# One 512 KB broadcast load per pair, or four of 128 KB: the spread inverses of path A

## The chip, the cores and the metric

The kernel runs on one core of a Trainium2 chip. The metric is device time in microseconds (us) of a whole execution; lower is better. The core has five instruction streams: TensorE (PE, matmuls), VectorE (DVE), ScalarE (ACT), GpSimd (POOL) and SyncE (SP). In this kernel SP issues all the transfers, and 16 DMA engines carry them.

## What is computed

Two attention layers over the same input (2048 tokens, width 448, 16 heads of 28) are mixed by a gate. The change touches the first one, path A, at its last division:

```python
# path A, per head h: linear attention with a softmax feature map
phi_q = concat(softmax(q @ w_phi), softmax(-(q @ w_phi)))     # 56 features
phi_k = concat(softmax(k @ w_phi), softmax(-(k @ w_phi)))
num = phi_q @ (phi_k.T @ v)
den = phi_q @ phi_k.sum(axis=tokens) + 1e-6
o   = num / den                       # the change is in how 1/den is spread
a   = concat_heads(o) @ wo
# path B: full softmax attention of the same input, b
out = g * a + (1 - g) * b             # g = sigmoid(x . gate_w)
```

## The kernel before

Everything is float32; most products are split into a high and a low part (three passes of matmuls). The program has three stretches. The first (to about 205 us) projects q and k of path B and accumulates keys and values of path A. The second (205 to about 350 us) finishes path A: 16 token tiles of queries (`pq`), their features, the numerators, the division, the output projection (`poa`), and then the values of path B (`pvb`). The third (350 us to the end) is path B's softmax attention. Matmuls of a running maximum (`pmd`, `pmb`, line 260, which ACT and DVE reduce at lines 264 and 265) are spread through the second stretch.

PE, DVE, ACT and POOL run in the order in which the Python code emits instructions. SP is not on that list: the library's scheduler sets the order of the transfers. Each transfer signals its completion on one of eight semaphore lanes, DMAHW0 to DMAHW7, taken in turn; a transfer whose lane is still held by an unfinished one waits at SP, and all behind it wait too.

Path A's division works on pairs of token tiles, `tb` = 0 to 7, 256 tokens each. Per pair:

- `numer` (PE, line 529) makes two tiles `pn` of 128 partitions by 512. Rows 32j to 32j+27 are a head's numerators, row 32j+28 its denominators. ACT copies them to `oUa` (`normalize1`, line 381).
- SP takes the four rows of denominators of each tile out of `oUa` into the small tile `dena` (line 384), so that many partitions hold them.
- `normalize2`: DVE takes the reciprocals (line 389); SP writes them to the DRAM tile `rda`, 4 rows of 1024 numbers (line 393), and loads `rda` back into `rsa`, 128 partitions of 1024 numbers, each of the four rows spread over 32 partitions (line 394). This load is what is changed.
- `normalize3`: DVE multiplies `oUa` by `rsa` (line 400). `normalize4`: ACT makes the high part of the result `oTa` (line 408), POOL the low part (line 409). `out_a` (line 538) projects it.

The loop at line 703 places these steps: the step with line 389 comes two turns after line 381, and line 400 two turns after that, with other work of DVE between. `rsa` has two buffers, `oUa` three. Path B uses the same functions with n = 1 (`rsb`, one tile, 256 KB), where line 400 runs on POOL.

Of the kernel before, what the change touches and what calls it, by code (L numbers as in the profile page):

```python
# [41 lines left out]
def gated_mix_kernel(ctx, tc, xT, wqkB, wvB, wvA, wkAT, wqAT, phi, woA, woB,  # L42
# [7 lines left out]
    nc = tc.nc  # L50
# [336 lines left out]
    def normalize2(pool, oU, den, nm, n):  # L387

        nc.vector.reciprocal(den, den)
        rd = dr.tile([4, n * 512], F32, tag=f"rd{n}", name=f"rd{nm}", bufs=2)  # L390
        rs = pool.tile([P, n, 512], F32, tag="rs", name=f"rs{nm}", bufs=n)
        for k in range(n):
            nc.sync.dma_start(rd[:, k * 512:(k + 1) * 512], den[:, k, :])
        nc.sync.dma_start(rs.rearrange("p n q -> p (n q)"),
                          rd.unsqueeze(1).to_broadcast([4, 32, n * 512]))
        return oU, rs

    def normalize3(oU, rs, n):
# [304 lines left out]
    for i in range(2 * NT + 11):  # L703
        t, q = i, i - NT
# [44 lines left out]
        if y >= 6 and y % 2 == 0 and tb - 3 < 8:  # L749
            num[tb - 3] = normalize2(ta, *num[tb - 3], f"a{tb - 3}", 2)  # L750
# [293 lines left out]
    def finish(gq, s):  # L1044
# [8 lines left out]
        def f2():  # L1053
            st["n"] = normalize2(late_p, *st["n"], f"b{gq}", 1)
# [189 lines left out]
```

## Time and profile before

| | us |
|---|---|
| median of 3 runs | 977.87 (977.84 to 979.14) |
| the profiled execution, whole | 978.57 |
| its span, first to last instruction | 976.8 |
| PE busy | 969.2 (99%) |
| ACT busy | 751.8 (77%) |
| DVE busy | 715.7 (73%) |
| POOL busy | 227.8 (23%) |
| 16 DMA engines, mean share | 27% |

The granted clock of TensorE is 1.0 throughout. A span is read from the first to the last instruction, and what the runtime adds around it (978.57 less 976.8, 1.77 us) is in the run's time. "Idle before" in the rows below is time in which an engine had nothing running, with what ended it behind the arrow; a chain of waits follows the program back from its last instruction to whatever released each step. "SPq" marks SP's issue of a transfer, so its duration is issue and not movement.

### The profile page before, as it was taken

How to read it: one execution, taken by the hardware profiler on the slowest of the kernel's cores; microseconds unless marked ns; L12 is line 12 of the kernel's file. 1: busy time of each engine (PE TensorE's matmuls, PEld its weight loads, DVE VectorE, ACT ScalarE, POOL GpSimd, SP SyncE). 2: the span in 40 equal slices, each digit the busy share in tenths (PEclk: the TensorE clock that was granted, in tenths of full speed). 3: DMA queues.
4: the chain of work that ended last, by engine and by line, in shares of the span. 5: the costliest groups of instructions: out<-in, count | busy, mean ns of one | idle time of the engine just before them, and what ended most of it. 6: DMA issues, size and time to landing. Idle time of an engine off the chain costs nothing.

```text
span 976.8 us, 22541 instructions
## 1 busy us (share of the span) xinstructions
PE 969.2 (99%) x8510; PEld 600.1 (61%) x8510; DVE 715.7 (73%) x1338; ACT 751.8 (77%) x1442; POOL 227.8 (23%) x236
## 2 busy tenths in 40 slices
PE   9999999999999999999999999999999999999998
PEld 8777877787777655555555555545555555555555
DVE  5567767788845678888888888888888888885112
ACT  4455655577865688989888898888988989887662
POOL 1135445577634800021001001011011011010010
PEclk9999999999999999999999999999999999999999
DMA  8873110023233333021132021122231222100441
GB/s 305 303 259 118 40 53 33 29 58 94 73 108 109 101 111 132 26 59 53 57 94 74 30 61 49 59 78 69 65 83 46 65 59 72 34 21 32 143 151 57
DMA packets 56140, 84.49 MB, mean 86 GB/s; under 512 B 17216, under 2 KB 23984, under 8 KB 56032
## 3 DMA queue, kind: packets, MB, share of 16 engines
q1 hardware_dynamic: 56032, 83.06, 27.1%
q8 instruction: 67, 1.10, 0.4%
q14 instruction: 41, 0.34, 0.1%
HBM read 54.86 MB, written 27.78 MB: 85 GB/s over the span
## 4 chain that ended last, share of the span: by engine, by line
PE 91%; DMA 5%; DVE 2%; ACT 1%; issue 1%; SPq 0%; DVEq 0%; ACTq 0%
PE g L863 29%; PE pv L1008 27%; PE pqk L109 4%; PE pk L127 4%; PE pva L127 4%; PE g L288 4%; PE poa L109 3%; PE pmd L260 3%; PE pob L109 3%; PE pq L109 3%; PE pvb L127 2%; PE pvb L109 2%; DMA rsa<-rda 2%; DMA qkd<-ev 1%; DMA xraw<-in_xT_dram 1%
## 5 line engine op out<-in xcount | busy, mean ns | idle before, releaser
L871 ACT ACTIVATE p<-g 128x512 f32<-128x512 f32 x1020 | 525.6, 608 | 82.7 <-PE g L863 82.4
L295 DVE TENSOR_REDUCE part<-g 128x1 f32<-128x512 f32 x704 | 442.3, 684 | 84.1 <-PE g L288 80.8
L863 PEld LDWEIGHTS g<-qst,kst 32*128 32x128 f32 x3060 | 220.9, 182 | 215.4 <-DVE part L295 195.1
L863 PE MATMUL g<-qst,kst 32*128 32x512 f32 x3060 | 337.6, 419 | 0.1
L1008 PE MATMUL pv<-p,vb 128*32 128x512 f32 x2048 | 273.0, 604 | 0.0
L288 PE MATMUL g<-kc,qc 28*128 28x512 f32 x704 | 233.3, 495 | 0.0
L265 DVE CUSTOM_DVE_ANT_0 rl<-pmb,rl 128x512 f32<-128x512 f32 x160 | 103.4, 683 | 49.6 <-ACT rl L264 49.6
L400 POOL TENSOR_TENSOR oUb<-oUb,rsb 128x512 f32<-128x512 f32 x15 | 19.3, 1289 | 489.9 <-DMA rsb<-rdb 366.2
L264 ACT ACTIVATE rl<-pmd 128x512 f32<-128x512 f32 x160 | 87.3, 601 | 31.1 <-PE pmb L260 29.3
L288 PEld LDWEIGHTS g<-kc,qc 28*128 28x128 f32 x704 | 86.2, 181 | 0.2
L1008 PEld LDWEIGHTS pv<-p,vb 128*32 128x32 f32 x2048 | 40.5, 108 | 66.2 <-issue 64.9
L109 PE MATMUL pqk<-XH,wB 128*128 128x512 f32 x192 | 59.4, 397 | 0.8 <-DVE ev L569 0.8
L568 ACT CAST ev<-pqk 128x512 fp32r<-128x512 f32 x28 | 16.0, 589 | 38.5 <-PE pqk L109 22.5
L1019 DVE SCALAR_TENSOR_TENSOR acc<-pob,gate,acc 128x448 f32<-128x448 f32 x12 | 8.2, 684 | 48.3 <-PE pob L109 48.3
L109 PE MATMUL poa<-woA_s,oTa 128*128 128x448 f32 x192 | 43.6, 375 | 0.0
L260 PE MATMUL pmb<-kp,qp 28*128 28x512 f32 x160 | 41.7, 495 | 0.4
L109 PEld LDWEIGHTS pqk<-XH,wB 128*128 128x128 f32 x192 | 35.3, 188 | 9.9 <-issue 1.5
L569 DVE TENSOR_TENSOR ev<-pqk,ev 128x512 fp32r<-128x512 f32 x28 | 18.9, 690 | 30.5 <-ACT ev L568 30.4
L260 PE MATMUL pmd<-kp,qp 28*128 28x512 f32 x160 | 39.9, 494 | 0.0
L127 PE MATMUL pk<-wkA_s,XH 128*128 128x448 f32 x128 | 39.4, 381 | 0.0
L109 PEld LDWEIGHTS poa<-woA_s,oTa 128*128 128x128 f32 x192 | 34.8, 188 | 6.6 <-issue 2.5
L109 PE MATMUL pq<-wqA_s,XH 128*128 128x448 f32 x128 | 37.3, 374 | 0.8 <-ACT oUa L381 0.8
(158 smaller groups left out, 1052.2 us busy)
## 6 DMA issues: line engine op xcount, KB each, us to landing
qkd<-ev SPq DMA_DIRECT2D x28, 512.0 KB
qst<-qkd SPq DMA_DIRECT2D x64, 112.0 KB
kst<-qkd SPq DMA_DIRECT2D x64, 112.0 KB
od<-oTb SPq DMA_DIRECT2D x48, 112.0 KB
rsa<-rda SPq DMA_DIRECT2D x8, 512.0 KB
oL<-od SPq DMA_DIRECT2D x8, 512.0 KB
rsb<-rdb SPq DMA_DIRECT2D x15, 256.0 KB
gad<-ga SPq DMA_DIRECT2D x16, 224.0 KB
```

The lines of the kernel that those rows point to most:

```text
L109: nc.tensor.matmul(dst, l, r, start=i == 0, stop=i == len(todo) - 1)
L127: nc.tensor.matmul(dst[:, :n], l, r, start=i == 0, stop=i == len(todo) - 1, skip_group_check=True)
L260: nc.tensor.matmul(pm[j], qc[js, qt * P:(qt + 1) * P], kc[js, :], start=True, stop=True, tile_position=(32 * i, 0))
L264: nc.scalar.activation(rl, pm[i], AF.Relu)
L265: nc.vector.tensor_tensor_reduce(rl, pm[2 + i], rl, 1.0, LOWEST, ALU.add, ALU.max, part[:, col + i:col + i + 1])
L288: nc.tensor.matmul(pm, mxs[("qc", gq)][js, qt * P:(qt + 1) * P], mxs[("kc", gq // NQ, kb)][js, :], start=True, stop=True, tile_position=(3 ...
L295: nc.vector.tensor_reduce(part[:, col:col + 1], pm, AX.X, ALU.max)
L400: (nc.gpsimd if n == 1 else nc.vector).tensor_mul(oU, oU, rs)
L569: nc.vector.tensor_sub(e[:, 1, :], pq, f32(e[:, 0, :]))
L863: nc.tensor.matmul(st[j], kst_of[(gq // NQ, kt // 4)][js, k, (kt % 4) * P:(kt % 4 + 1) * P], qst_of[gq][js, q, :], start=n == 0, stop=n == ...
L871: nc.scalar.activation(p, st[j], AF.Exp, scale=SCALE)
L1008: nc.tensor.matmul(pv[32 * j:32 * j + 32, :], vb[kt // 8][:, kt % 8, 4 * g + j, :], pt[j], start=kt == 0, stop=kt == NT - 1, tile_position ...
```

## The change

For pairs (n = 2, path A alone) the load of line 394 is replaced by four loads, one per source row j: 32 copies of row j of `rda` (4 KB) go to partitions 32j to 32j+31 of `rsa`. The bytes are the same, 8 times 512 KB. Path B keeps its single load. Lines after 394 move down by five.

```diff
         for k in range(n):
             nc.sync.dma_start(rd[:, k * 512:(k + 1) * 512], den[:, k, :])
-        nc.sync.dma_start(rs.rearrange("p n q -> p (n q)"),
-                          rd.unsqueeze(1).to_broadcast([4, 32, n * 512]))
+        rows = rs.rearrange("p n q -> p (n q)")
+        if n == 2:
+            for j in range(4):
+                nc.sync.dma_start(rows[32 * j:32 * j + 32],
+                                  rd[j:j + 1].to_broadcast([32, n * 512]))
+        else:
+            nc.sync.dma_start(rows, rd.unsqueeze(1).to_broadcast([4, 32, n * 512]))
         return oU, rs
```

The order of PE, DVE, ACT and POOL stays as it was; only what they wait for is renamed. SP has 24 more transfers, and its order shifts around them. Three places matter.

SP, from pair 0's load to pair 1's (`qp` are queries for the running maximum, `dena` and `rda` as above; the brackets name the lanes and engines waited for). Before:

```order
L394 DMA rsa_2538<-rda_2537 128x1x1024 [waits DMAHW7_49,DMAHW4_49,DMAHW3_49]
L176 DMA qp_1_2800<-qkd 28x512 [waits DMAHW0_49,PE_49]
L176 DMA qp_1_2800<-qkd 28x512 x2
L393 DMA rda_2673<-dena_2570 4x32x16 [waits DMAHW5_49,DVE_49]
L393 DMA rda_2673<-dena_2570 4x32x16 [waits DMAHW6_49]
L384 DMA dena_2706<-oUa_2703 128x1x16 [waits Activation_49] x2
L176 DMA qp_1_2800<-qkd 28x512 [waits DMAHW7_49]
L394 DMA rsa_2674<-rda_2673 128x1x1024 [waits DMAHW4_49,DMAHW3_49,DMAHW0_49]
```

With the change:

```order
L397 DMA rsa_2538<-rda_2537 32x1024 [waits DMAHW7_49,DMAHW4_49,DMAHW3_49]
L397 DMA rsa_2538<-rda_2537 32x1024 [waits DMAHW0_49]
L397 DMA rsa_2538<-rda_2537 32x1024 x2
L176 DMA qp_1_2806<-qkd 28x512 [waits PE_49]
L176 DMA qp_1_2806<-qkd 28x512
L393 DMA rda_2676<-dena_2573 4x32x16 [waits DMAHW5_49,DVE_49]
L393 DMA rda_2676<-dena_2573 4x32x16 [waits DMAHW6_49]
L384 DMA dena_2712<-oUa_2709 128x1x16 [waits DMAHW7_49,Activation_49]
L384 DMA dena_2712<-oUa_2709 128x1x16 [waits DMAHW0_49,Activation_49]
L176 DMA qp_1_2806<-qkd 28x512 [waits DMAHW1_49]
L397 DMA rsa_2677<-rda_2676 32x1024 [waits DMAHW6_49,DMAHW5_49,DMAHW2_49]
```

The single load took lane 7, and the last `qp` before pair 1's load waited for that lane. Now the four take lanes 7, 0, 1 and 2, and the transfers that come next on these lanes wait for the pieces.

SP again, in the second half of the stretch, where `kt` (keys for the running maximum) stood ahead of pair 7's `rda`. Before:

```order
L176 DMA kt_1_3683<-qkd 28x512 [waits DMAHW4_49,Pool_49]
L176 DMA kt_1_3683<-qkd 28x512 [waits DMAHW5_49]
L393 DMA rda_3619<-dena_3479 4x32x16 [waits DMAHW6_49,DVE_49]
L393 DMA rda_3619<-dena_3479 4x32x16 [waits DMAHW7_49]
```

With the change:

```order
L176 DMA kt_1_3707<-qkd 28x512 [waits DMAHW1_49,Pool_49]
L393 DMA rda_3640<-dena_3500 4x32x16 [waits DMAHW2_49,DVE_49]
L393 DMA rda_3640<-dena_3500 4x32x16 [waits DMAHW3_49]
L176 DMA kt_1_3707<-qkd 28x512 [waits DMAHW4_49]
```

The second `kt`, which waited for lane 5 and with it for pair 6's load, now comes after both `rda`.

DVE, the multiplication of pair 0. Before, and then with the change:

```order
L400 TENSOR_TENSOR oUa_2458<-oUa_2458,rsa_2538 128x1024 [waits DMAHW7_49,DMAHW0_49]
```

```order
L405 TENSOR_TENSOR oUa_2458<-oUa_2458,rsa_2538 128x1024 [waits DMAHW2_49,DMAHW7_49,DMAHW1_49,DMAHW0_49]
```

The one instruction now waits for four lanes, one for each piece, where one of its two was the whole load's.

## The prediction

> **What bounds the kernel now.** I read the page's busy times and its chain first: what does PE leave idle, and does the changed load stand on the path?
>
> ```profile
> span 976.8 us, 22541 instructions
> PE 969.2 (99%) x8510; PEld 600.1 (61%) x8510; DVE 715.7 (73%) x1338; ACT 751.8 (77%) x1442; POOL 227.8 (23%) x236
> PE 91%; DMA 5%; DVE 2%; ACT 1%; issue 1%; SPq 0%; DVEq 0%; ACTq 0%
> ```
>
> PE bounds it. The chain charges `rsa<-rda` with 2%, which is two loads of 8.8 us; but PE worked through most of that, so this share is no gain. What a faster load is worth is only the PE time that its lateness costs. Who waits for it is in the list of waits of the second stretch, 205 to 325 us, and in its rows on SP (total, times, longest; the last row is the stretch itself, with the busy times of PE, its weight loads, DVE, ACT and POOL):
>
> ```profile
> DVE oUa L400 <- DMA rsa<-rda: 4.8, 3, 2.4
> ACT oTa L408 <- DVE oUa L400: 1.5, 2, 0.8
> SPq L176 <- DMA rsa<-rda: 7.7, 3, 4.7
> 205.00:325.00 120.00, 118.55 (x859) 92.41 (x839) 81.51 (x187) 87.90 (x166) 72.55 (x66) 1.00 0.27 83
> ```
>
> Three of the eight multiplications find DVE idle for the load, 4.8 us together; PE idles 120 - 118.55 = 1.45 us in the whole stretch. A matmul that waits for a buffer can also be shown as busy, so I compare the starts of PE's groups around the two long waits. Timeline of pair 0:
>
> ```profile
> 217.78 8.81 DMA rsa<-rda
> 224.52 0.18 DVE L445 TENSOR_TENSOR fsumq<-fsumq,featq 128x16 f32<-128x16 f32 x1
> 226.69 1.22 DVE L400 TENSOR_TENSOR oUa<-oUa,rsa 128x1024 f32<-128x1024 f32 x1 [1.98 <-DMA rsa<-rda]
> 227.94 1.14 ACT L408 CAST oTa<-oUa 128x512 fp32r<-128x512 f32 x2 [0.80 <-DVE oUa L400]
> 229.21 0.50 PE L260 MATMUL pmd<-kp,qp 28*128 28x512 f32 x2
> 229.63 1.10 PE L260 MATMUL pmb<-kp,qp 28*128 28x512 f32 x2
> 230.66 1.09 PE L529 MATMUL pn<-fT,KV 57*32 57x256 f32 x32
> 231.68 2.93 PE L109 MATMUL poa<-woA_s,oTa 128*128 128x448 f32 x12
> 234.45 1.03 PE L516 MATMUL pft<-ident,featq 128*128 128x128 f32 x8
> ...
> 243.80 0.51 PE L260 MATMUL pmd<-kp,qp 28*128 28x512 f32 x2
> 244.24 1.09 PE L529 MATMUL pn<-fT,KV 57*32 57x256 f32 x32
> 245.27 2.72 PE L109 MATMUL poa<-woA_s,oTa 128*128 128x448 f32 x12
> 247.82 1.03 PE L516 MATMUL pft<-ident,featq 128*128 128x128 f32 x8
> ```
>
> The last four rows are the same work undisturbed: 0.44 us from the maximum's matmuls to `pn`, 2.55 us from `poa` to `pft`. Behind the late load these are 1.45 and 2.77: **1.01 + 0.22 = 1.23 us** lost. `pmb` wanted a buffer that DVE empties after line 400. And pair 4:
>
> ```profile
> 263.54 8.83 DMA rsa<-rda
> 269.65 0.35 DVE L389 RECIPROCAL dena<-dena 128x32 f32<-128x32 f32 x1
> 272.39 1.23 DVE L400 TENSOR_TENSOR oUa<-oUa,rsa 128x1024 f32<-128x1024 f32 x1 [2.39 <-DMA rsa<-rda]
> 273.65 1.14 ACT L408 CAST oTa<-oUa 128x512 fp32r<-128x512 f32 x2 [0.70 <-DVE oUa L400]
> 274.69 1.13 ACT L519 COPY fT<-pft 128x384 f32<-128x384 f32 x3
> 275.22 0.68 PE L109 MATMUL pvb<-wvB_s,XH 128*128 128x448 f32 x2 [0.18 <-ACT fT L519]
> ```
>
> Line 408 is 0.70 us late for line 400, line 519 behind it, and PE waits **0.18 us**. Pair 1 waits 0.43 us (4.8 less the two) and costs PE nothing visible. So the lateness is worth 1.23 + 0.18 = 1.41 us, about 0.3 us of PE for each us that DVE waits.
>
> **The change, part by part.** First, how fast the load is and why.
>
> ```profile
> 222.00:223.00 1.00, 0.25 (x3) 0.01 (x1) 1.00 (x5) 1.00 (x3) 1.00 (x2) 1.00 0.82 154
> 224.00:225.50 1.50, 1.50 (x8) 1.13 (x6) 0.64 (x3) 0.50 (x2) 0.93 (x2) 1.00 0.25 101
> ```
>
> The last two columns are the mean share of the 16 DMA engines and GB/s. From 224.0 to 225.5 the big load is nearly alone: share 0.25, so four engines' worth of work, at 101 GB/s, 25 each. A microsecond after three 28-partition loads went out (222 to 223) the share is 0.82. So transfers of some 28 partitions reach most engines and the present load does not: its source is written as 4 rows by 32 copies. On this the Trainium skill's page DMA: Bandwidth & Descriptors has a rule (Why a DMA increments its semaphore by 16 and not by 1, and Rules for kernel authors): the number of engines is the largest up to 16 that divides the outermost size of both sides, so a leading 4 confines a transfer to 4. The trace's 0.25 agrees; by that rule each piece, 32 on both sides, gets 16.
>
> Landing. A spread load of about this kind is the `kt` pair:
>
> ```profile
> 316.36 0.73 SPq L176 DMA_DIRECT2D kt<-qkd  x2
> 318.29 2.65 POOL L206 TENSOR_TENSOR kp<-kp,kt 28x512 fp32r<-28x512 f32 x2 [1.96 <-DMA kt<-qkd]
> L176 SPq DMA_DIRECT2D kt<-qkd x16: 306/356/385, 43.3 to 316.7; - x16
> L394 SPq DMA_DIRECT2D rsa<-rda x8: 522/534/546, 217.8 to 297.7; - x8
> ```
>
> From the first issue to the user is 1.93 us for two of 56 KB, or about 1.57 us from the second issue. Issue costs 0.36 us (28 partitions) to 0.53 us (the present load). Four pieces: the last is issued 1.1 to 1.6 us after the first, and lands 1.6 us later, plus the time for 512 KB less the 112 KB of the pair: 400 KB at 154 GB/s is 2.7 us if nothing overlaps, nearly nothing if movement runs under the issues. That is 2.7 to 5.9 us, and I take 4 us against 8.8, because the pieces move while later ones are issued. DVE wants the data 224.70 - 217.78 = 6.9 us after the issue in pair 0 and 270.00 - 263.54 = 6.5 us in pair 4. Both ends of the estimate meet that, so all three waits go.
>
> What then is next: line 400 of pair 0 starts at 224.7, but the reduction after it needs ACT's copy at 226.15 (`pcq`), so DVE is ahead by 227.83 - 226.15 = 1.68 us, not 1.98. The second line 265 then ends at 230.17 - 1.68 = 228.5, before PE asks at 229.21. That suffices for the 1.01 us; line 409 on POOL moves up too, for the 0.22.
>
> ```profile
> 225.62 0.53 ACT L421 COPY pcq<-pq 128x448 f32<-128x448 f32 x1 [1.12 <-PE pq L109]
> 227.83 0.61 DVE L423 TENSOR_REDUCE extq<-pcq 128x16 f32<-128x448 f32 x1
> 230.10 0.08 DVE L265 DVE_READ_ACCUMULATOR2_ANT part<- 128x1 f32 x1
> ```
>
> The lost side, with the row of SP's next transfer after pair 0's load:
>
> ```profile
> 220.32 1.19 SPq L176 DMA_DIRECT2D qp<-qkd  x3
> ```
>
> 24 more issues at 0.36 to 0.53 us are 8.6 to 12.7 us of SP, 1.1 to 1.6 us per pair for whatever is queued behind: `qp`, `dena`, `rda`, `gad`. I cost this at nothing. Behind pair 0's load the next transfer goes out only at 220.32, because it waits for PE, and SP is free from 218.31; behind pair 5's, `gad` is next, whose `ga` has three buffers. Without that cover it would be 1.1 to 1.6 us on a chain, 0.5 us of PE by the ratio above. SP also gains: 7.7 us of lane waits on the long load go, so pair 1's load leaves earlier. Three more lane waits on line 400 are some 20 ns each (the event rows on DVE last 21 ns): hidden.
>
> Sum: span 976.8 - 1.4 = 975.4. That execution took 978.57 whole, while the median is 977.87; I take the difference off the median: 977.87 - 1.4 = **976.4 us**. PE is busy nearly everywhere after 235 us, so the lead should last to the end.
>
> **The rivals.**
>
> *More than the sum* (975.4). Two further rows of losses, and the row of line 400 over all pairs (shortest, median, longest; first and last start):
>
> ```profile
> 299.60 0.49 PE L260 MATMUL pmd<-kp,qp 28*128 28x512 f32 x2
> 300.45 0.67 PE L109 MATMUL pvb<-wvB_s,XH 128*128 128x448 f32 x2 [0.34 <-ACT ga L544]
> L400 DVE TENSOR_TENSOR oUa<-oUa,rsa x8: 1217/1220/1736, 226.7 to 308.5; 128x1024 f32<-128x1024 f32 x8
> ```
>
> PE loses another 0.4 us at 300.45 us, where `pvb` follows the maximum's matmuls after 0.85 us instead of 0.44, behind ACT's line 544; one line 400 took 1.74 us where 1.22 is the median. With both, 1.4 + 0.4 + 0.5 = 2.3, and some small waits on top: about 2.5. Against it: the 300.45 gap follows no wait for the load.
>
> *One row cannot feed 16 engines* (slower). Now four engines read four rows, 25 GB/s from each row; with the change 16 engines read the same 4 KB. No row of the trace shows a row read by more than one engine. If a row gave r GB/s in all, the last piece would land 524 KB / r + 2 us after the issue: 8.8 us, as now, at r = 77, so below that the change loses. At 50 GB/s it is 12.5 us, 3.7 later; the present slack of the pairs (from landing to line 400, by the issues and starts of both) is about -2.0, -0.4, 2.8, 3.0, -2.4, 1.2, 1.6, 2.0, so the added waits come to about 3 x 3.7 + 0.9 + 0.7 + 2.5 + 2.1 + 1.7 = 19 us, and at 0.3 to 0.6 us of PE each 6 to 11 us: about 986. At the 25 GB/s that one engine shows, 21 us per load would exceed the 11 us between loads, and 8 x 21 us against the 91 us from the first to the last makes some 1050. For it: identical addresses. Against it: one engine alone already drew 25 GB/s from one row without a sign of slowing.
>
> *The pieces serialize* (977.9 to 979.3). If each piece ran on the engines that the load has now, at 101 GB/s in turn, the last would land between now and 1.6 us later, and three waits longer by 1.6 cost 4.8 x 0.3 = 1.4 us. Against it stands the 0.82 of smaller transfers. The Trainium skill's page DMA: Bandwidth & Descriptors (Rules for kernel authors) says that cutting a transfer into disjoint halves of the partitions is no help, since both halves already spread over all 16 engines; its premise is not what the row of 0.25 shows of this load.
>
> *SP becomes the late one* (about 981). If the 1.6 us reach line 393 of the next pair each time, 7 x 1.6 x 0.3 = 3.4 us. The shifted order, `qp` and `gad` between pieces, speaks for it; the idle stretches of SP against it.
>
> **How the numbers follow.** About 0.2% (2 us) is what a measurement of this kernel can tell from no change. The forecast has 50%; its gain is 1.4 us with an uncertainty of about 0.6, and I let 14 of the 50 fall beyond 2 us. More than the sum 22% (faster); one row 16% (slower); serialized 4% (same); SP late 8% (slower). Faster: 14 + 22 = 36%. Same: 36 + 4 = 40%. Slower: 16 + 8 = 24%. The range reaches from 974.6, which leaves some 4% of the larger gains out, to 984, which takes in SP late and mild forms of the one-row case and leaves some 13% above. The forecast's own range is 975.6 to 977.2.
>
> **What would show it.** Right: DMA share well above 0.25 behind each issue; line 405 (was 400) without idle time on the load; `pn` 0.44 us after the maximum's matmuls at pair 0; SP without waits on `rsa`. The forecast is wrong if `rsa` lands more than 6.5 us after its first issue, if DVE waits for it in more than the three pairs, or if PE's lead of 1.4 us at 276 us is gone at the end.

## The result, and the profile after

| | before | after |
|---|---|---|
| median, us | 978.74 (977.1 to 984.2, 21 runs) | 976.76 (975.81 to 978.36, 21 runs) |
| the profiled execution, whole | 978.57 | 976.53 |
| its span | 976.8 | 974.7 |

The changed kernel is faster: the ratio of the times is 0.9976, with a 95% interval of 0.9967 to 0.9985, that is 2.35 us (1.5 to 3.2). The medians differ by 1.98 us and the two profiled executions by 2.04 us. The predicted 976.4 us lies 0.4 us under the measured median.

First the page of the kernel after: span, busy time per engine, and the chain that ended last, by engine.

```profile
span 974.7 us, 22584 instructions
PE 967.9 (99%) x8510; PEld 600.0 (62%) x8510; DVE 716.0 (73%) x1338; ACT 751.6 (77%) x1442; POOL 229.9 (24%) x236
PE 92%; DMA 4%; DVE 2%; ACT 1%; issue 1%; POOL 0%; SPq 0%; DVEq 0%; ACTq 0%; POOLq 0%
```

PE is 1.3 us less busy with the same 8510 matmuls, since some of its busy time before was waiting. The chain still charges DMA with 4%, where it was 5%, though the load of line 397 now keeps nobody waiting: a share of the chain says what ran last, not what could be gained.

The list of waits on DVE in the second stretch (205 to 325 us) of the kernel after, in full; columns are total, times and longest, in us:

```profile
DVE rl L265 <- ACT rl L264: 28.7, 19, 4.7
DVE extq L428 <- ACT pcq L426: 4.4, 5, 1.9
DVE featq L448 <- ACT featq L439: 2.6, 4, 1.1
```

The row of line 400 on `rsa`, 4.8 us before, has no successor. The 7.7 us that SP waited for lanes held by `rsa` are gone from SP's list too. A window of the same trace while pair 2's four pieces move (length, busy time of PE, its weight loads, DVE, ACT and POOL, the granted clock, the DMA share and GB/s):

```profile
236.90:239.50 2.60, 2.60 (x18) 2.44 (x16) 2.29 (x6) 2.60 (x5) 2.08 (x4) 1.00 0.86 264
```

Where the single load kept a quarter of the 16 engines busy at 101 GB/s, 0.86 of them are busy here at 264 GB/s. Part of this is a `gad` transfer of 224 KB, issued at 235.79 us just ahead of the pieces; the pieces by themselves are measured further down, where the landing is. Pair 0 in the timeline of the kernel after (start, duration, engine and line):

```profile
217.49 1.77 SPq L397 DMA_DIRECT2D rsa<-rda  x4
...
224.39 1.23 DVE L405 TENSOR_TENSOR oUa<-oUa,rsa 128x1024 f32<-128x1024 f32 x1
...
228.94 0.50 PE L260 MATMUL pmd<-kp,qp 28*128 28x512 f32 x2
...
229.38 1.09 PE L534 MATMUL pn<-fT,KV 57*32 57x256 f32 x32
...
230.40 2.71 PE L109 MATMUL poa<-woA_s,oTa 128*128 128x448 f32 x12
...
232.95 1.03 PE L521 MATMUL pft<-ident,featq 128*128 128x128 f32 x8
```

DVE's multiplication has no idle time before it. `pn` follows the maximum's matmuls after 0.44 us, where it took 1.45, and `pft` follows `poa` after 2.55, where it took 2.77. At the maximum's matmuls PE is 0.27 us ahead of the kernel before (229.21 there), at `pn` 1.28 (230.66), at `pft` 1.50 (234.45). Pair 4 in the timeline of the kernel after:

```profile
268.41 1.16 DVE L405 TENSOR_TENSOR oUa<-oUa,rsa 128x1024 f32<-128x1024 f32 x1
...
270.85 2.69 PE L109 MATMUL poa<-woA_s,oTa 128*128 128x448 f32 x12
273.38 0.57 PE L109 MATMUL pvb<-wvB_s,XH 128*128 128x448 f32 x2
...
275.74 0.50 PE L260 MATMUL pmd<-kp,qp 28*128 28x512 f32 x2
```

And the two rows of the kernel before that stand against `poa` and the last row:

```profile
272.35 2.69 PE L109 MATMUL poa<-woA_s,oTa 128*128 128x448 f32 x12
...
277.65 0.50 PE L260 MATMUL pmd<-kp,qp 28*128 28x512 f32 x2
```

From `poa` to `pvb` PE now takes 2.53 us, where it took 2.87 (272.35 to 275.22). So pair 4 gives back 0.34 us, not the 0.18 us of idle time. Undisturbed, `pvb` starts 0.16 us before the row of `poa` ends (270.85 + 2.69 = 273.54), and an idle time is counted only from that end. At 275.74 the lead is 1.91 us. Of this, 0.28 us were there before anything that was changed. The first `pq` of the stretch, in the kernel before:

```profile
213.62 0.64 PE L109 MATMUL pq<-wqA_s,XH 128*128 128x448 f32 x2
```

and in the kernel after:

```profile
213.34 0.64 PE L109 MATMUL pq<-wqA_s,XH 128*128 128x448 f32 x2
```

That leaves 1.91 - 0.28 = **1.63 us** that the change gained inside the stretch, and it holds: PE's groups at 349 us start 1.86 us earlier (1.58 without the 0.28). This difference of starts, from 213 us to the maximum's matmuls at 276 to 278 us, is the number by which the experiments are compared below, because it leaves out how an execution began.

### The profile page after: what moved, and what is told of

Its sections match the earlier page's. It is cut to its first block, busy times and chain, and to the rows that moved or that the text cites. A ratio compares the mean times of both kernels' runs of the same rounds, so it can differ in the third digit from the quotient of the medians.

```text
span 974.7 us, 22584 instructions
## 1 busy us (share of the span) xinstructions
PE 967.9 (99%) x8510; PEld 600.0 (62%) x8510; DVE 716.0 (73%) x1338; ACT 751.6 (77%) x1442; POOL 229.9 (24%) x236
## 4 chain that ended last, share of the span: by engine, by line
PE 92%; DMA 4%; DVE 2%; ACT 1%; issue 1%; POOL 0%; SPq 0%; DVEq 0%; ACTq 0%; POOLq 0%
PE g L868 29%; PE pv L1013 27%; PE poa L109 4%; PE pk L127 4%; PE pva L127 4%; PE g L288 3%; PE pqk L109 3%; PE pmd L260 3%; PE pq L109 3%; PE pob L109 3%; PE pvb L127 2%; PE pvb L109 2%; DMA qkd<-ev 2%; PE pft L521 1%; DMA xraw<-in_xT_dram 1%; PE pkv L473 1%
```

## The experiments

The theory: what counts is how many of the 16 engines a transfer reaches, which the number of rows at the head of its source limits; the wait for the late load then costs PE 1.23 us at pair 0 and 0.2 to 0.3 at pair 4, and nothing elsewhere. The main rival: four transfers move faster because they are four (four queue entries, four lanes), whatever their shape. Each timed kernel is compared with runs of the kernel before on the same chip; the edits are shown against the kernel after unless another is named.

### Four pieces that each keep the four rows

The pieces are cut by columns, so that each still has 4 rows of 32 copies.

```diff
-            for j in range(4):
-                nc.sync.dma_start(rows[32 * j:32 * j + 32],
-                                  rd[j:j + 1].to_broadcast([32, n * 512]))
+            for c in range(0, 1024, 256):
+                nc.sync.dma_start(rows[:, c:c + 256],
+                                  rd[:, c:c + 256].unsqueeze(1).to_broadcast([4, 32, 256]))
```

> Four transfers per pair again, but each takes all four source rows and a quarter of the columns (source 4 x 32 x 256), so the number of transfers, lanes and issues is that of the change, and the leading 4 that of before. Theory (engines: the gain comes from reaching 16 engines instead of 4): DMA share stays near 0.25 behind the issues, the last piece lands 8.8 to 10.4 us after the first issue, DVE waits for rsa in at least the same three pairs, 5 to 10 us in all; time 0 to 1.5 us above before. Rival (queue: the gain comes from cutting the transfer up, with its four lanes and the new order on SP): DVE's waits shrink and the time is 1 to 2.4 us below before.

Measured: 979.67 us (11 runs) against 978.19 (29 runs), ratio 1.0014 (1.0006 to 1.0023). Two windows of its trace while the pieces of pair 0 move:

```profile
224.00:225.00 1.00, 1.00 (x5) 0.93 (x6) 1.00 (x2) 1.00 (x3) 1.00 (x2) 1.00 0.26 93
225.00:226.00 1.00, 1.00 (x7) 0.91 (x6) 0.54 (x3) 0.40 (x1) 0.42 (x2) 1.00 0.28 98
```

And its timeline, the issue and the user of pair 0's load:

```profile
218.66 2.35 SPq L397 DMA_DIRECT2D rsa<-rda  x4
...
227.49 1.23 DVE L405 TENSOR_TENSOR oUa<-oUa,rsa 128x1024 f32<-128x1024 f32 x1 [1.87 <-DMA rsa<-rda]
```

The share stays at 0.26 to 0.28 and 93 to 98 GB/s, the user starts 8.8 us after the first issue, as with one transfer, and DVE waits three times, 6.0 us in all. PE loses 0.70 us in the stretch; that the times are above before by 0.14% says little, since the kernel before shows as much against itself below. Four transfers alone bring nothing, and the rival falls. The pieces of the change are faster because of their shape.

### Two pieces of two rows

```diff
-            for j in range(4):
-                nc.sync.dma_start(rows[32 * j:32 * j + 32],
-                                  rd[j:j + 1].to_broadcast([32, n * 512]))
+            for j in (0, 2):
+                nc.sync.dma_start(rows[32 * j:32 * j + 64],
+                                  rd[j:j + 2].unsqueeze(1).to_broadcast([2, 32, n * 512]))
```

> Two transfers per pair, two source rows each (source 2 x 32 x 1024). Engines theory: each runs on two engines at 25 GB/s each, the same two for both, so 512 KB at 50 GB/s is 10.5 us and the last lands about 12.5 us after the issue; by the slack of the pairs DVE waits about 19 us in all, and at 0.3 to 0.6 us of PE for each the time is 6 to 11 us above before; DMA share near 0.125. Queue rival: two pieces give about half of the gain of four, 1 us below before.

Measured: 1007.53 us (5 runs), ratio 1.0299 (1.028 to 1.0318), 29 us slower. The whole trace's waits on `rsa`:

```profile
DVE oUa L405 <- DMA rsa<-rda: 39.5, 8, 7.4
```

Windows of the same trace, the first while pair 0's load is alone, the second of 10 us behind it:

```profile
227.00:228.00 1.00, 1.00 (x7) 0.93 (x6) 0.00 (x0) 0.00 (x0) 0.00 (x0) 1.00 0.12 49
...
235.00:245.00 10.00, 10.00 (x72) 7.48 (x72) 4.75 (x13) 5.75 (x12) 5.70 (x6) 0.76 0.15 52
```

And pair 0 in its timeline:

```profile
217.36 1.08 SPq L397 DMA_DIRECT2D rsa<-rda  x2
...
228.81 0.50 PE L260 MATMUL pmd<-kp,qp 28*128 28x512 f32 x2
230.90 1.23 DVE L405 TENSOR_TENSOR oUa<-oUa,rsa 128x1024 f32<-128x1024 f32 x1 [6.62 <-DMA rsa<-rda]
...
233.84 1.40 PE L260 MATMUL pmb<-kp,qp 28*128 28x512 f32 x2 [4.53 <-DVE part L265]
235.17 1.96 PE L534 MATMUL pn<-fT,KV 57*32 57x256 f32 x32
237.06 3.98 PE L109 MATMUL poa<-woA_s,oTa 128*128 128x448 f32 x12
240.88 1.03 PE L521 MATMUL pft<-ident,featq 128*128 128x128 f32 x8
```

The direction is the theory's: a share of 0.12 at 49 GB/s is two engines' worth, and the load takes 13.5 us from issue to user where 12.5 was expected. The Trainium skill's page DMA: Bandwidth & Descriptors (Why a DMA increments its semaphore by 16 and not by 1) gives the number of engines as the largest up to 16 that divides the outermost size of both sides; the shares 0.12 and 0.25 for outermost sizes 2 and 4, and 0.90 for one piece with 32 (measured where the landing is), agree with 2, 4 and 16.

The size was badly off: I expected 6 to 11 us. The waits come to 39.5 us instead of 19. That each late load also pushes back the next would fit it, and is not tested by itself: the eight loads are issued 14.0 to 16.7 us apart here, where the kernel before has 9.1 to 13.4. And the long wait at pair 0 costs PE nearly its whole length. From `pmd` to `pn` PE takes 6.36 us instead of 0.44, which is 5.9 lost; then `pn` to `poa` takes 1.89 instead of 1.02 and `poa` to `pft` 3.82 instead of 2.55, which is 2.1 more, lost without any wait, in a window whose granted clock is 0.76. Pair 0 thus lost 8.0 us of PE behind a wait of 6.62, where the rate of 0.3 that I had worked out from waits of 2 us would give 2.0.

### Only the pairs that waited, and only the others

Three pairs had waited before (0, 1 and 4). In the first kernel only these are cut, in the second only the other five.

```diff
-        if n == 2:
+        if nm in ("a0", "a1", "a4"):
```

```diff
-        if n == 2:
+        if n == 2 and nm not in ("a0", "a1", "a4"):
```

> Four transfers for pairs 0, 1 and 4 alone, the three whose line 400 waited in the profile of before; pairs 2, 3, 5, 6 and 7 keep the single load. Engines theory, where only the three waits cost: the whole gain of the change, 1.4 to 2.4 us below before. Queue rival: three eighths of it, 0.5 to 0.9 us below. If only the executions that were not profiled wait in other pairs, something between.

> The complement: four transfers for pairs 2, 3, 5, 6 and 7, the single load for pairs 0, 1 and 4. Engines theory: the three waits stay (4.8 us of DVE in the profile), so no gain, within 0.4 us of before. Queue rival: five eighths of the gain, 0.9 to 1.5 us below before.

Measured: the three pairs 977.99 us (12 runs), ratio 0.9996 (0.9987 to 1.0006); the five others 977.72 (11 runs), ratio 0.9995 (0.9986 to 1.0003). The times tell the two apart neither from each other nor from the kernel before. The traces do. The three pairs leave no wait on `rsa`, and PE gains 1.63 us in the stretch, as with the whole change. With the five others PE is 0.08 us later, and two waits remain, in that kernel's timeline:

```profile
225.98 1.23 DVE L405 TENSOR_TENSOR oUa<-oUa,rsa 128x1024 f32<-128x1024 f32 x1 [1.26 <-DMA rsa<-rda]
...
272.48 1.22 DVE L405 TENSOR_TENSOR oUa<-oUa,rsa 128x1024 f32<-128x1024 f32 x1 [3.21 <-DMA rsa<-rda]
```

What pair 0 gains there (1.98 us of wait before), pair 4 loses (2.39 before), and PE with them: 0.74 us from the maximum's matmuls to `pn` at pair 0 against 0.81 from `poa` to `pvb` at pair 4. By the traces the gain sits in the three pairs. The timed runs of the first kernel do not show it (0.4 us where 1.6 was expected), so they are repeated next, beside a measure of what the comparison itself can tell.

### The change, the three pairs and the kernel before, once more

The third of these is the kernel before without any edit: what it shows is the error of the comparison.

> The change once more, beside the three-pairs kernel and the kernel before on one chip, since single executions scatter by about 1 us and the change's 2.35 us below before (interval 1.5 to 3.2) was measured apart from the experiments. Engines theory with the cost read from the profile: 1.4 to 1.9 us below before. If pairs that do not wait in the profile wait in other executions: 2 to 2.4 us below, and lower than the three-pairs kernel of this job by 0.5 us or more.

> Four transfers for pairs 0, 1 and 4 alone, again. Its first profile gained 1.58 us of PE in the second stretch against before, but its timed runs only 0.4 us (interval -1.3 to +0.6). Engines theory: 1.4 to 1.9 us below before, no different from the change in this job by more than 0.4 us. Rival (the other five pairs carry part of the gain): 0 to 1 us below before, 0.5 us or more above the change.

> The kernel before, unchanged, as a measure of what this comparison shows for nothing: within 0.1% of itself (1 us). Its second profile tells whether the early part (PE 0.3 us earlier at 40 us in the profile of the change, ahead of everything that was changed) and the three waits of 4.8 us differ between executions: the early part is expected to differ by some tenths of a us, the waits to be again in pairs 0, 1 and 4 and 4 to 6 us in all.

| on one chip, beside 35 runs of the kernel before (978.36) | median, us | ratio (95%) | PE's gain in the stretch by the trace |
|---|---|---|---|
| the change | 977.04 (11 runs) | 0.9984 (0.9973 to 0.9995) | 1.63 |
| three pairs | 977.12 (12 runs) | 0.9992 (0.9983 to 1.0001) | 1.64 |
| the kernel before, again | 978.84 (12 runs) | 1.0014 (1.0004 to 1.0024) | -0.04 |

By its ratio the unedited copy came out 1.4 us slower than itself, with an interval that leaves 1 out; by the medians it is 0.5 us. So I take these intervals for too narrow: what is under some 0.14% can be a matter of how the executions fell. By the medians the change is 1.8 us faster than the copy and the three pairs 1.7 us. The times do not tell the change and the three pairs apart: their medians differ by 0.1 us, their ratios by 0.8 us, and that second figure is what the rival of the other five pairs expected. The traces of both repeat 1.63 and 1.64 us, and neither has a wait of DVE on `rsa`. The three pairs' kernel still has this row among SP's waits in the stretch:

```profile
SPq L176 <- DMA rsa<-rda: 7.1, 2, 5.5
```

In this execution it keeps nearly all of SP's waits for the long load, in its first one only 1.1 us of them, and PE gains as much as with the change both times (1.64 and 1.63): the 7.7 us of lane waits were worth nothing to PE. The copy of the kernel before has two waits of DVE, where three were expected:

```profile
DVE oUa L400 <- DMA rsa<-rda: 4.5, 2, 2.3
```

They are those of pairs 0 and 4 (2.15 and 2.31 us). Pair 1 does not wait, and PE is no earlier for it (-0.04): its 0.43 us in the first profile were worth nothing, as the prediction had it.

### Eight pieces

Each row in two halves, 64 transfers of 64 KB: does the issue cost anything?

```diff
-                nc.sync.dma_start(rows[32 * j:32 * j + 32],
-                                  rd[j:j + 1].to_broadcast([32, n * 512]))
+                for c in (0, 512):
+                    nc.sync.dma_start(rows[32 * j:32 * j + 32, c:c + 512],
+                                      rd[j:j + 1, c:c + 512].to_broadcast([32, 512]))
```

> Eight transfers per pair, each row in two halves of 512 columns: all 16 engines still, twice the issues of the change (56 more than before, 0.3 to 0.45 us each, 17 to 25 us of SP). Engines theory with SP off the path: the last lands about 1.7 us later than with four, 5 us after the first issue and still inside the 6.5 us that the pairs allow, so no waits of DVE and the same time as the change, 1.4 to 2.4 us below before. Rival (SP's issue and the eight lanes are near the path): waits on SP for lanes appear, DVE waits again, and the time is at or above before.

Measured: 977.27 us (11 runs), ratio 0.9987 (0.9977 to 0.9996), the same as four pieces within what the times can tell. The issues of its trace (count; shortest, median and longest duration in ns; first and last start):

```profile
L398 SPq DMA_DIRECT2D rsa<-rda x64: 307/419/1084, 217.8 to 297.7; - x64
```

SP issues for 3.6 to 4.4 us per pair, and no wait of DVE on `rsa` appears. PE gains 1.16 us in the stretch, 0.47 less than with four pieces, and the trace shows where it is lost. Pair 0 in its timeline (line 452 of POOL works on the features of the queries, line 406 is the multiplication):

```profile
224.88 0.94 POOL L452 TENSOR_TENSOR featq<-featq,fsumq 128x448 f32<-128x448 f32 x1 [0.58 <-DVE fsumq L451]
224.93 1.98 DVE L406 TENSOR_TENSOR oUa<-oUa,rsa 128x1024 f32<-128x1024 f32 x1 [0.19 <-DMA rda<-dena]
```

The same two in the kernel after, where the multiplication starts at 224.39 and takes 1.23 us:

```profile
224.55 1.87 POOL L451 TENSOR_TENSOR featq<-featq,fsumq 128x448 f32<-128x448 f32 x1 [0.58 <-DVE fsumq L450]
```

Of these two, the one that starts first keeps its pace, and the other takes 0.75 to 0.93 us longer. With four pieces DVE starts first; with eight it starts 0.19 us later, just behind POOL. This is so in pairs 0 to 3, and PE is late behind two of them: from `poa` to `pft` at pair 0 it takes 2.75 us (2.55 in the kernel after), and from the maximum's matmuls at 265.09 to `pn` 0.65 instead of 0.44, behind an ACT row that waited for pair 3's multiplication:

```profile
263.22 1.15 ACT L414 CAST oTa<-oUa 128x512 fp32r<-128x512 f32 x2 [0.20 <-DVE oUa L406]
```

These are 0.41 of the 0.47 us. So four pieces are enough, and the trace shows no cost of SP's time. Why DVE starts 0.19 us later is not shown; that it now has more lanes to wait for is a guess.

### How long a load takes, by itself

In the kernel after, DVE asks for the load only when it is there, so a row does not show when it landed. Here the multiplication is placed directly behind the reciprocals of its own pair; DVE then stands waiting whenever the load lands. The first kernel is the kernel before with this edit, the second the kernel after with the same.

```diff
             num[tb - 3] = normalize2(ta, *num[tb - 3], f"a{tb - 3}", 2)
+            num[tb - 3] = normalize3(*num[tb - 3], 2)
...
-        if y >= 8 and y % 2 == 0 and y < NT and tb - 4 < 8:
-            num[tb - 4] = normalize3(*num[tb - 4], 2)
...
-        if y >= NT and y % 2 == 0 and tb - 4 < 8:
-            num[tb - 4] = normalize3(*num[tb - 4], 2)
```

> A ruler, not a candidate: the kernel before, with line 400 of each pair moved to directly behind line 389 on DVE, so that DVE stands waiting when the load lands and the landing shows as the start of line 400. Engines theory: single load lands 7.5 to 9 us after its issue in all eight pairs (8.8 with other traffic in between); the kernel is some tens of us slower for the standing DVE.

> The same ruler on the change: the last of the four pieces lands 3 to 4.5 us after the first issue in all eight pairs (DMA share fell to nothing 3 us after it in the profile of the change), so about 5 us sooner than the single load. If the landing were 6 us or more, the three waits would have gone for another reason than the landing.

Measured: 1057.6 and 1026.9 us (one run each), slow as they must be with DVE standing still. The timeline of the one with the single load:

```profile
217.60 0.53 SPq L394 DMA_DIRECT2D rsa<-rda  x1
...
225.82 1.23 DVE L400 TENSOR_TENSOR oUa<-oUa,rsa 128x1024 f32<-128x1024 f32 x1 [10.86 <-DMA rsa<-rda]
```

and of the one with four pieces:

```profile
217.56 1.77 SPq L397 DMA_DIRECT2D rsa<-rda  x4
...
222.02 1.22 DVE L405 TENSOR_TENSOR oUa<-oUa,rsa 128x1024 f32<-128x1024 f32 x1 [7.10 <-DMA rsa<-rda]
```

That is 8.2 us from the first issue to the user against 4.5. Over the eight pairs the single load takes 7.6 to 8.8 us and the four pieces 4.1 to 4.8. The four are a little above the 4 us that I took and the 3 to 4.5 expected here, and well below the 6.9 and 6.5 us at which DVE wants the data in pairs 0 and 4. Two windows of the second trace, in which no other transfer is under way:

```profile
218.50:218.95 0.45, 0.45 (x4) 0.42 (x3) 0.00 (x0) 0.45 (x2) 0.00 (x0) 1.00 0.90 146
218.60:219.60 1.00, 1.00 (x7) 0.66 (x5) 0.00 (x0) 0.64 (x2) 0.00 (x0) 1.00 0.97 266
```

Nothing of the load moves before 218.5 us, and the second piece was issued 0.43 us behind the first, so the first window is as good as the first piece alone. It reads one 4 KB row, and 0.90 of the 16 engines are busy at 146 GB/s: one row does feed nearly all engines at once.

### Path B's load too

```diff
-        if n == 2:
+        if n:
```

> The change, with path B's 15 loads of 256 KB cut into four rows too (45 more transfers). There POOL waits for rsb, 366 us idle in 11 waits, but POOL is busy 23% and its result is due one turn later, so nobody on the path waits for it. Theory (only lateness that reaches PE counts): the landing falls from 5.0 us to about 3.5 us in the third stretch and the time stays that of the change within 0.5 us, 1.4 to 2 us below before. Rival (faster loads help wherever an engine waits for them): a further 1 us or more; and if SP is near the path there: slower than the change by 1 us or more.

Measured: 977.25 us (12 runs), ratio 0.9986 (0.9977 to 0.9995), against 978.02 (17 runs): not told apart from the change alone. Path B's load does become faster. From issue to user it took 4.96 us in the kernel before (407.63 to 412.59), and in this one's timeline 3.52:

```profile
406.40 1.70 SPq L397 DMA_DIRECT2D rsb<-rdb  x4
...
409.92 1.28 POOL L405 TENSOR_TENSOR oUb<-oUb,rsb 128x512 f32<-128x512 f32 x1 [43.61 <-DMA rsb<-rdb]
```

PE's gain in the second stretch is 1.62 us, as before, and nothing is added: the multiplication there is POOL's. POOL does wait for the load (43.61 us in this row), but the lists of waits have no engine that waits for what POOL makes of it. No kernel of these beats the change.

## Why the prediction was right

**The time.** That 976.4 us comes so near to 976.76 is partly luck. The base, 977.87 us from three runs, was 0.9 us under the median of 21 runs (978.74), and the gain of 1.4 us was 0.6 under the difference of the medians (1.98); the two errors offset each other. What stands by itself is the gain in the stretch, 1.41 us predicted and 1.63 measured.

**How fast the load is.** Right. The step that took 4 us (2.7 to 5.9) for the landing is answered by 4.1 to 4.8; the share of 0.25 turned into 0.90 to 0.97. The rate in that step, 154 GB/s, came from a window in which the old load moved as well; the pieces alone reach 266. What I had as the explanation, the leading 4 of the source, is what the two kernels with leading 4 and leading 2 single out.

**All three waits go.** Right. DVE's list has no row of `rsa` left, and none of the four other traces with those pairs cut into four has one.

**Pair 0, 1.01 + 0.22.** Right to the hundredth: the lead goes from 0.27 to 1.28 at `pn` and to 1.50 at `pft`.

**Pair 4, 0.18.** The mechanism was right and the term too small: 0.34. I had compared starts at pair 0, but at pair 4 took the idle time from the row, which leaves out the 0.16 us by which `poa` and `pvb` overlap undisturbed. By starts the sum would have been 1.23 + 0.34 = 1.57 us, and the five traces with pairs 0, 1 and 4 cut into four show 1.62 to 1.64.

**SP, nothing.** Right for 24 more issues. The three-pairs kernel, with 9 more, gains no more and no less, so neither the added issues nor the vanished lane waits count. The eight pieces, with 56 more, lose 0.47 us of the gain, but by DVE's place beside POOL.

**The lead lasts to the end.** Right: 1.91 us at 276 us, 1.86 at 349, 2.1 in the spans.

**The rivals.** *More than the sum* had the right size for the first comparison (2.35 us), but its mechanism did not show up. Its first item, PE's gap behind ACT's line 544, is still there in the kernel after, now line 549:

```profile
PE pvb L109 <- ACT ga L549: 0.3, 1, 0.3
```

Its second, the multiplication of 1.74 us, is gone (the longest now takes 1226 ns), and PE's starts show no gain for it; there too POOL had started first, 0.29 us ahead. What the comparison shows above 1.6 us is not seen in the traces: 0.28 us of the profiled execution arose before the first changed instruction, and the unedited copy moved by 1.4 us. *One row cannot feed 16 engines* is refuted by the 146 GB/s of one piece from one row. Its formula gave 8.8 us at 77 GB/s. A load at 49 GB/s did come in the two-row kernel, for another reason (two engines); there the rival's price was 6 to 11 us and 29 were lost. What failed in that price is the 0.3 to 0.6 us of PE per us of wait: the ratio comes from waits of about 2 us, of which most was covered; at the 6.62 us of pair 0 PE lost 8.0. *The pieces serialize* and *SP becomes the late one* did not come.

**What stays open.** How much of the timed 2.35 us is the change. The traces say 1.6, the repeat 1.6 (0.5 to 2.6), the difference to the copy 1.8. The first timed runs of the three-pairs kernel (0.4 us) fit only if the scatter of the copy, 1.4 us, is allowed for. One thing on record may point to the other five pairs after all. Of the 117 executions on record with their clock that keep the single load in pairs 2, 3, 5, 6 and 7 (the kernel before, its copy and the three pairs), 17 have a mean granted clock of 0.996 to 0.998 and take 979.8 to 982.4 us, five of them among the 24 of the three pairs; of the 77 that cut these five pairs too (the change, eight pieces, path B too, the five others, four by columns), none has. No such execution was profiled, so its cause stays open. Without them the first runs of the three pairs still lie only 0.6 us below before, and in the repeat the change and the three pairs both 1.1.

## What to carry to other kernels

Look at the mean DMA share while a broadcast load is alone: 0.25 went with a source that leads with 4. Cut into pieces that lead with 32 copies the load lands in little more than half the time, whereas as many pieces with the leading 4 gain nothing. Price a late load by the starts of the bounding engine's groups against the same work undisturbed, not by the chain's share and not by idle time alone, and do not carry a price per us from a short wait to a long one. A faster load pays where somebody waits for it: in the traces the other five pairs and path B's load got faster for nothing. One trace per kernel does not settle whether the five pairs are worth nothing in every execution.

## What the runs showed of the hardware

The granted clock falls when PE stands still. In the kernel with the single load and the early multiplication PE ran out of work at about 220.0 us, by its timeline:

```profile
219.53 0.50 PE L260 MATMUL pmd<-kp,qp 28*128 28x512 f32 x2
230.27 1.48 PE L260 MATMUL pmb<-kp,qp 28*128 28x512 f32 x2 [10.24 <-DVE part L265]
```

Windows of the same trace:

```profile
222.60:223.60 1.00, 0.00 (x0) 0.00 (x0) 0.00 (x0) 0.00 (x0) 0.00 (x0) 1.00 0.27 111
223.60:224.60 1.00, 0.00 (x0) 0.00 (x0) 0.00 (x0) 0.00 (x0) 0.00 (x0) 0.62 0.24 98
224.60:225.60 1.00, 0.00 (x0) 0.00 (x0) 0.00 (x0) 0.00 (x0) 0.00 (x0) 0.50 0.06 25
...
232.00:234.00 2.00, 2.00 (x34) 0.88 (x19) 1.97 (x5) 0.65 (x1) 2.00 (x3) 0.50 0.32 84
```

The clock is full for 3.6 us, goes down within the next one, and is still at half while PE is busy again at 232 us. So a wait of this length is paid twice, which fits the 2.1 of the 8.0 us at pair 0 of the two-row kernel, where PE had stood for 4.53 us and the clock of the window behind it is 0.76. The Trainium skill's page TensorE: Matmul & The Clock Gate (What's actually happening) states half rate after at least one idle window of about 3.4 us; the trace agrees.

The same skill's page DMA: Bandwidth & Descriptors (Rules for kernel authors) advises against cutting a transfer by partitions, as every part would use the same 16 engines. Here the uncut transfer had a share of four engines, and the cut took the landing from 7.6 to 8.8 us down to 4.1 to 4.8; the measurement decides.
